# Queue positions of Q's weight loads and of the second gate/up group in a linear-attention and ReGLU block

## The chip, the cores and the metric

The kernel runs on one core of one Trainium2 chip. Its engines work from separate instruction queues: TensorE (PE) multiplies matrices into PSUM, VectorE (DVE) and ScalarE (ACT) take results out of PSUM and do elementwise work, GpSimd (POOL) does elementwise work in SBUF, and SyncE (SP) only issues DMA transfers. Each queue is worked off in the order in which it was written; an engine that waits holds everything behind it. The metric is the device time of one execution in microseconds (us); smaller is better.

## The reference

One transformer block on 2048 tokens (S) of width 1024 (D), in bf16:

```python
x = A_x
h = x + _A_ref(_layernorm(x), A_wqkv, A_wo)
h2 = h + _B_ref(_layernorm(h), B_W_gate, B_W_up, B_W_down)

# _A_ref: 32 heads of 32, linear attention, phi(t) = (t + 1 if t > 0 else exp(t)) + 1e-6
q, k, v = split(x @ wqkv)
kv  = einsum("sd,se->de", phi(k), v)          # per head, summed over all tokens
z   = sum over tokens of phi(k)
o   = (phi(q) @ kv) / (phi(q) @ z + 1e-6)
return o @ wo

# _B_ref
return (relu(x @ W_gate) * (x @ W_up)) @ W_down     # width 3584 inside
```

K and V of all tokens must be known before the first token's attention can be computed; Q is first needed after that.

## The kernel before

**Products.** The large products are written as Strassen-like quads (`Quad`): a two-by-two block product in seven half-size products m = 1 to 7 instead of eight, in Winograd's form. Each needs sums and differences of the blocks of both operands. Those of the weights are made by `WForms.sums` (four DVE subtractions of 128 x 2048 elements for each of K, V and Q; m = 4 to 7 use them) and, for gate and up, by `GW.sums` (four of 128 x 1024 elements); those of the activations by `left_sums`. A quad's own copies and additions (`fork`, `snap`, and the functions in its `out` table) fall to ACT and DVE.

**Stages.**
1. x is loaded in 16 tiles of 128 tokens. `Norm` computes mean and variance of a tile (on DVE for one half, on ACT for the other), scales it on POOL (`finish`, line 677) and has SP transpose it by a DMA (`dma_start_transpose`, line 682) into `XI`. The first two tiles, 0 and 8, are transposed on TensorE instead, so SP transposes 14 tiles of x.
2. The loop of line 868 runs over token pairs p = 1 to 7 (tiles p and p + 8): a quad for K, one for V, and the accumulation of kv and z (`kv_acc`). The norm of the tiles of pair p + 2 is started in the background of pair p (line 872), so tiles 7 and 15 are started in pair 5.
3. The Q quads (`q_quad`) follow: four for token half-block s = 0 and four for s = 1. `Tile_` computes attention for a tile of tokens: `group` the division, with an x tile loaded again for the residual and a DMA transpose of o at its end; `wo` the output product and the residual sum; `norm` (line 1033) the second layer norm, whose normalized tile `hn` is again transposed by SP into `XI` (line 1041). There are eight such tiles in each of s = 0 and s = 1, so 32 transposes in this stage.
4. Gate and up (`gu_halves`, then `gu_quad`) run over `order` (line 1188): `n` counts its entries, the first four of which are s = 0 with weight columns fc = 0 to 3. Gate and up weights come in groups of two columns fc, four DMAs each of 512 KB (`load_group`). Group 0 is loaded ahead of the Q quads; group 1, for fc = 2 and 3, is written in the source behind the first entry's quads (line 1239) and goes into memory in which Q's weights stood, half of it free once the second Q quad of s = 1 is done and the other half after the fourth.
5. The down product follows from spilled and reloaded operands, to the end.

**Order.** No engine runs the source's order. `Plan` records every operation as a node with the nodes whose data it needs (`preds`), the time that it holds its engine, and its latency. `order` works out for every node how late it may start (`late`); `schedule` then goes through model time and gives each engine, whenever it is free, the one of its ready nodes with the smallest `late` (TensorE: the earliest in source order within a window). A node that has no urgent use is thus taken early when its engine is free in the model and its inputs are there. A load is ready as soon as its memory is free, and up to 120 us ahead of its `late`; a load that isn't urgent is held only until the model's wire is free:

```python
if v.late - max(clock[e], v.ready) > 6000.0:
    v.ready = max(v.ready, wire - 2000.0)
```

The queue of SP comes out of this too, and so does the place of the weight differences among DVE's other work. On the chip the order of each queue is fixed; the waits between engines come from the data alone.

**Names that the change touches.** `Plan.take` makes the nodes. `W_ORDER` and `WQ.load(k, h)` are the four loads of Q's weights, 512 KB each; in the source they stand at line 875, after K's quad of p = 3. `WQ.sums()`, Q's four differences, is put in the background at p = 6 (line 873).

Of the kernel before, what the change touches and what calls it, by code (L numbers as in the profile page):

```python
# [32 lines left out]
class Plan:  # L33
# [12 lines left out]
    class Engine:  # L46
        def __init__(self, plan, name):
            self._plan, self._name = plan, name
# [3 lines left out]

    def __init__(self, nc):
        self.nc, self.nodes, self.state, self.cache = nc, [], {}, {}
        for e in ("tensor", "vector", "scalar", "gpsimd", "sync"):
            setattr(self, e, Plan.Engine(self, e))

# [33 lines left out]
    def cost(self, eng, op, out, ins, k):  # L91

        n = self.free(out)
        if eng == "tensor":
            return max(n / 2.4, 98.0) if op == "matmul" else 80.0, 160 + self.SEM
        if op == "dma_start" and eng == "gpsimd":
            return 1000.0, 2.0 * self.wire(out) + 4500.0
        if op == "dma_start" and eng == "gpsimd":
            return 1000.0, 2.0 * self.wire(out) + 2500.0
        if eng == "sync":  # L100
            return (1250.0, 2350.0) if op == "dma_start_transpose" else (500.0, self.wire(out) + 2200.0)
        acc = 85.0 if k.get("accum_out") is not None else 0.0
        psum = any(a.space == PSUM for a in ins)
        if eng == "vector":
            narrow = all(self.nbytes(a) == 2 and a.space != PSUM for a in (out, *ins) if self.free(a) > 1)
            mode = {"tensor_tensor": 2, "tensor_scalar": 4, "memset": 2}.get(op, 1) if narrow else 1
            if ins:
                n = max(n, self.free(ins[0]))
            return n / (0.96 * mode) + 69 + acc, 95 + self.SEM
        if eng == "scalar":  # L110
            return n / 1.2 + (51 if psum else 93) + 2 * acc, 105 + self.SEM
        return n * 1.15 + 100, 60 + self.SEM

    def take(self, eng, op, args, k):
        outs, ins = [], []
        for i, a in list(enumerate(args)) + list(k.items()):
            if hasattr(a, "ap") and hasattr(a, "offset"):
                (outs if i in (0, "out", "accum_out") else ins).append(a)
        out = outs[0]
        accumulates = k.get("accum_op") is not None or op == "matmul" and not k.get("start", True)  # L120
        nodes = self.nodes
        call = lambda: getattr(getattr(self.nc, eng), op)(*args, **k)  # L122
        hold, lat = self.cost(eng, op, out, ins, k)
        if nodes and nodes[-1].open and op == "matmul":
            v = nodes[-1]
            v.hold += hold
        else:
            v = Plan.Node()
            v.eng, v.calls, v.preds, v.hold, v.lat, v.dma = eng, [], set(), hold, lat, 0.0
            if op == "dma_start":  # L130
                v.dma = self.wire(out) * (2.0 if eng == "gpsimd" else 1.0)
            nodes.append(v)
        v.calls.append(call)
        v.open = op == "matmul" and not k.get("stop", True)
        me = len(nodes) - 1
        for a in ins + (outs if accumulates else []):
            if a.space == DRAM and a.tensor.name.startswith("in_"):
                continue
            name, gs = self.granules(a)
            last, readers = self.state.setdefault(name, ({}, {}))  # L140
            for q in gs:
                w = last.get(q)
                if w is not None:
                    v.preds.add(w)
                readers.setdefault(q, set()).add(me)
        for a in outs:
            name, gs = self.granules(a)
            if eng == "tensor" and not accumulates:

                per = 2048 // self.G  # L150
                gs = [per * b + i for b in sorted({q // per for q in gs}) for i in range(per)]
            last, readers = self.state.setdefault(name, ({}, {}))
            for q in gs:
                w = last.get(q)
                if w is not None:
                    v.preds.add(w)
                r = readers.pop(q, None)
                if r:
                    v.preds |= r
                last[q] = me  # L160
        v.preds.discard(me)

    def cut(self):

        if self.nodes:
            self.nodes[-1].open = False
# [128 lines left out]
def chain_of(*fs):  # L295

    if not fs:
        return None

    def f():  # L300
        fs[0]()
        return chain_of(*fs[1:])

    return f
# [155 lines left out]
def block_kernel(ctx: ExitStack, tc: tile.TileContext, x, wqkv, wo, wg, wu, wd, out, H: int):  # L460
    nc = tc.nc
# [8 lines left out]
    ST = S // P  # L470
# [77 lines left out]
    hw, nc = nc, Plan(nc)  # L548
# [12 lines left out]
    W_ORDER = ((0, 0), (1, 0), (0, 1), (1, 1))  # L561
# [28 lines left out]
    WK, WV, WQ = WForms(84, D), WForms(112, 2 * D), WForms(56, 0)  # L590
# [34 lines left out]
    class Norm:  # L625
# [51 lines left out]
        def finish(self):  # L677
            self.rstd_()
            xn = self.xn
            nc.gpsimd.tensor_scalar(out=xn, in0=self.x, scalar1=self.negm[:], scalar2=self.rstd[:],  # L680
                                    op0=ALU.add, op1=ALU.mult)
            nc.sync.dma_start_transpose(out=XI[self.i][:, :, self.r:self.r + P], in_=xn)
            if self.t % NP + 2 < NP:
                load_x(self.t + 2)

# [182 lines left out]
    for p in range(1, NP):  # L868
        pk, kq = k_quad(p)
        if p > 1:  # L870
            q = 3 if p == 2 else p + 2
            tick.bg.extend([norm(q), None, norm(q + NP, True)] if q < NP else
                           [None, *WQ.sums()] if p == NP - 2 else [])
        qs.run(kq)
        if p == 3:
            for k, h in W_ORDER:
                WQ.load(k, h)
        v, vq = v_quad(p)
        ls = left_sums((p + 1) % NP * P, P)
        if p == 2:  # L880
            tick.bg.extend([norm(p + 2), norm(p + 2 + NP, True), None] + ls)
        else:
            tick.bg.extend(([None] * 3 if p == 1 else [None]) + ls)
        qs.run(vq)
        kv_acc(*pend.pop(0))
        pend.append((p, pk, v))
# [29 lines left out]
    def load_group(g):  # L916
        w = groups[g] = at(W_A[g], [2, KC, 2, 2 * P])
        for y, v in enumerate((wg_v, wu_v)):
            for h in range(2):
                nc.sync.dma_start(out=w[:, y, :, h, :], in_=v[:, :, h, g * 2 * P:(g + 1) * 2 * P])  # L920
# [42 lines left out]
    class Tile_:  # L963
# [69 lines left out]
        def norm(self):  # L1033
            lnv = scratch("lnv2", 1)
            nc.scalar.activation(out=lnv[:], in_=self.ss[:], func=ACT.Ln, bias=LN_EPS, scale=1.0 / D)
            rstd = scratch("rstd2", 1)
            nc.scalar.activation(out=rstd[:], in_=lnv[:], func=ACT.Exp, scale=-0.5)
            nc.gpsimd.tensor_scalar(out=self.hn, in0=self.h, scalar1=self.negm[:], scalar2=rstd[:],
                                    op0=ALU.add, op1=ALU.mult)
            c = slice(self.s * SW + self.tt * P, self.s * SW + (self.tt + 1) * P)  # L1040
            nc.sync.dma_start_transpose(out=XI[self.i][:, :, c], in_=self.hn)
            if self.i == 1 and (self.tt == 1 or self.tt > 1):
                n = 2 if self.tt == 1 else 1
                return (lag_s[0], chain_of(*left_sums(self.s * SW + (self.tt + 1 - n) * P, n * P)))

    lag_s = [3]
    tiles = [Tile_(s, i, tt) for s in range(NS) for tt in range(SW // P) for i in range(2)]

    def w(m, j):
# [16 lines left out]
    NTS = len(tiles) // 2  # L1066
# [162 lines left out]
    for n, (s, fc) in enumerate(order):  # L1229
        gw = forms[fc]  # L1230
        if n == 4:
            quads.flush()
            tick.drain()
        next_forms(n + 1)
        if n < 4:
            for q in gu_halves(s, fc, gw, five_banks):
                quads.run(q)
            if n == 0:
                load_group(1)
        else:  # L1240
            quads.run(gu_quad(s, fc, gw, four_pairs))
        if n in loads:
            load_group(loads[n])
        if 8 <= n < 8 + FH:
            wd_sums(n - 8)
        if 9 <= n < 13:
            spill(0, n - 9)
        if n == 24:
            r1 = at(164, [2, FQ, DW])
            for k in range(2):  # L1250
                nc.sync.dma_start(out=r1[:, k, :, :], in_=wd_pairs[:, 0, :, k, 0:DW])
            z1 = l1_part(0, 12)
        elif n == 26:
            z1 += l1_part(12, FH)
# [278 lines left out]
```

## Time and profile before

| | us |
|---|---|
| median of 4 runs | 728.9 |
| lowest and highest run | 728.73, 729.85 |
| the profiled execution's own time | 728.73 |
| its span in the profile | 727.0 |

The span is the time from the first to the last instruction in the trace; the 1.7 us beside it lie around it. Durations below are from this execution. In the profile's rows nearly all instructions stand under L122, the line through which `Plan` issues them, so they are told apart by engine, shape and tile names: `mem` is the one SBUF buffer, `psum` the PSUM banks, `tiny` small per-token values, `in_..._dram` the inputs. SPq rows are DMA issues: their length is the time that SP's queue was held, not the transfer's.

The stages by time, as the rows of TensorE, DVE and SP show them:

| us | stage |
|---|---|
| 0 to 22 | first loads, plain products of tiles 0 and 8 |
| 22 to 118 | K and V quads, p = 1 to 7 |
| 118 to about 195 | Q quads, and attention for s = 0 from 147 on |
| 195 to about 265 | gate and up begin, attention for s = 1 beside them |
| to 727 | gate, up and down |

Mean busy share of the 16 DMA engines in the 40 slices of 18.2 us begins with 9 9 5 5 2 0 4 5 2 3 9 9 tenths. From 74 to 87 us it is 0.22, from 87 to 113 us 0.01 or less.

### The profile page before, as it was taken

How to read it: one execution, taken by the hardware profiler on the slowest of the kernel's cores; microseconds unless marked ns; L12 is line 12 of the kernel's file. 1: busy time of each engine (PE TensorE's matmuls, PEld its weight loads, DVE VectorE, ACT ScalarE, POOL GpSimd, SP SyncE). 2: the span in 40 equal slices, each digit the busy share in tenths (PEclk: the TensorE clock that was granted, in tenths of full speed). 3: DMA queues.
4: the chain of work that ended last, by engine and by line, in shares of the span. 5: the costliest groups of instructions: out<-in, count | busy, mean ns of one | idle time of the engine just before them, and what ended most of it. 6: DMA issues, size and time to landing. Idle time of an engine off the chain costs nothing.

```text
span 727.0 us, 11235 instructions
## 1 busy us (share of the span) xinstructions
PE 715.1 (98%) x4163; PEld 396.9 (55%) x4163; DVE 563.0 (77%) x949; ACT 279.7 (38%) x544; POOL 80.5 (11%) x90
## 2 busy tenths in 40 slices
PE   8999999999999999999999999999999999999998
PEld 3444445444444444444444444444444688888887
DVE  6997645896897785575767968759668878999996
ACT  5778545666555443323333333333333220001100
POOL 2433000002202120000000000000000004101452
PEclk9999999999999999999999999999999999999999
DMA  9955205239945730456156485685592878877973
GB/s 306 242 119 120 40 1 168 66 79 245 197 104 146 145 87 0 123 147 180 51 147 195 151 250 163 189 254 180 160 290 70 267 260 200 229 272 236 235 88 59
DMA packets 156503, 117.40 MB, mean 161 GB/s; under 512 B 54944, under 2 KB 140192, under 8 KB 156320
## 3 DMA queue, kind: packets, MB, share of 16 engines
q1 hardware_dynamic: 148832, 113.01, 54.2%
q0 software_dynamic: 7616, 3.67, 4.7%
q8 instruction: 32, 0.52, 0.3%
q14 instruction: 23, 0.19, 0.1%
HBM read 70.52 MB, written 34.08 MB: 144 GB/s over the span
## 4 chain that ended last, share of the span: by engine, by line
PE 86%; DVE 5%; DMA 3%; ACT 3%; issue 1%; POOL 0%; SPq 0%; ACTq 0%; DVEq 0%
PE psum L122 86%; DVE mem L122 4%; ACT mem L122 3%; DMA mem<-mem 2%; DMA mem<-in_A_x_dram 1%; DVE tiny L122 0%; POOL mem L122 0%; SPq L122 0%; ACT tiny L122 0%; ACT psum L122 0%; ACTq L122 0%; DVEq L122 0%
## 5 line engine op out<-in xcount | busy, mean ns | idle before, releaser
L122 PE MATMUL psum<-mem 128*128 128x512 f16 (+4 forms) x4147 | 714.2, 335 | 7.9 <-ACT mem L122 3.3
L122 PEld LDWEIGHTS <-mem 128*128 128x128 f16 (+1 forms) x4163 | 396.9, 98 | 326.3 <-issue 9.5
L122 DVE TENSOR_TENSOR mem<-psum,mem 128x512 f32<-128x512 f32 (+2 forms) x240 | 187.3, 793 | 100.5 <-ACT mem L122 64.7
L122 DVE TENSOR_TENSOR mem<-mem 128x512 f16<-128x512 bf16 (+8 forms) x400 | 241.6, 644 | 15.5 <-DMA mem<-mem 7.9
L122 ACT COPY mem<-psum 128x512 f32<-128x512 f32 (+2 forms) x124 | 92.8, 750 | 210.8 <-PE psum L122 205.9
L122 ACT COPY psum<-psum 128x512 f32<-128x512 f32 (+1 forms) x68 | 49.1, 722 | 161.6 <-PE psum L122 159.5
L122 POOL DMA_DIRECT2D out_dram<-mem x28 | 34.1, 1302 | 413.8 <-DVE mem L122 413.7
L122 POOL TENSOR_SCALAR mem<-mem,tiny 128x1024 bf16<-128x1024 bf16 x30 | 39.6, 1321 | 196.4 <-ACT tiny L122 173.9
L122 ACT ACTIVATE mem<-psum 128x512 bf16<-128x512 f32 x90 | 53.8, 597 | 17.0 <-PE psum L122 16.4
L122 DVE SCALAR_TENSOR_TENSOR mem<-mem 128x512 bf16<-128x512 bf16 (+1 forms) x71 | 58.6, 825 | 1.3
L122 DVE SCALAR_TENSOR_TENSOR mem<-psum,mem 128x512 bf16<-128x512 f32 x66 | 45.4, 688 | 11.9 <-PE psum L122 7.9
L122 ACT ACTIVATE mem<-mem,tiny 128x1024 bf16<-128x1024 bf16 x25 | 28.6, 1145 | 10.6 <-DVE tiny L122 5.8
L122 DVE TENSOR_SCALAR mem<-mem 128x512 bf16<-128x512 bf16 (+1 forms) x49 | 16.4, 335 | 20.7 <-ACT mem L122 20.5
L122 ACT ACTIVATE mem<-mem 128x1024 bf16<-128x1024 f32 (+1 forms) x24 | 25.3, 1055 | 5.8 <-DVE mem L122 5.7
L122 DVE TENSOR_TENSOR mem<-psum,tiny 128x384 bf16<-128x384 f32 (+1 forms) x48 | 22.9, 508 | 5.3 <-ACT tiny L122 3.9
L122 ACT ACTIVATE tiny<-tiny 128x1 f32<-128x1 f32 (+2 forms) x112 | 22.7, 206 | 9.1 <-DVE tiny L122 6.3
L122 ACT ACTIVATE tiny<-psum 128x12 f32<-128x12 f32 (+1 forms) x48 | 8.2, 170 | 13.8 <-PE psum L122 13.4
L122 ACT CAST mem<-psum 128x512 bf16<-128x512 f32 x18 | 10.5, 582 | 2.8 <-PE psum L122 2.1
L122 DVE BATCH_NORM_STATS2 tiny<-mem 128x6 f32<-128x512 bf16 x14 | 9.0, 677 | 2.4 <-DMA mem<-in_A_x_dram 2.4
L122 POOL TENSOR_SCALAR tiny<-tiny 128x1 f32<-128x1 f32 x14 | 5.3, 378 | 25.7 <-ACT mem L122 18.1
L122 ACT ACTIVATION_READ_ACCUMULATOR mem<-mem,tiny 128x1 f32 x25 | 4.7, 189 | 0.0
L122 DVE TENSOR_SCALAR tiny<-tiny 128x1 f32<-128x1 f32 x16 | 3.4, 210 | 0.3
(18 smaller groups left out, 13.5 us busy)
## 6 DMA issues: line engine op xcount, KB each, us to landing
l_dram<-mem SPq DMA_DIRECT2D x98, 128.0 KB, 2.2
mem<-l_dram SPq DMA_DIRECT2D x12, 896.0 KB, 6.0
mem<-in_A_x_dram SPq DMA_DIRECT2D x32, 256.0 KB, 3.1
mem<-in_B_W_up_dram SPq DMA_DIRECT2D x14, 512.0 KB, 5.1
mem<-in_B_W_gate_dram SPq DMA_DIRECT2D x14, 512.0 KB, 4.1
mem<-in_B_W_down_dram SPq DMA_DIRECT2D x28, 256.0 KB, 3.7
r_dram<-mem SPq DMA_DIRECT2D x56, 128.0 KB, 2.0
mem<-r_dram SPq DMA_DIRECT2D x8, 896.0 KB, 5.2
```

The source lines that it names most:

```text
L122: call = lambda: getattr(getattr(self.nc, eng), op)(*args, **k)
```

## The change

`Plan` gets a field `behind`. While it is set to a node, every node of SP that is recorded has that node among its predecessors; with `chain` set, which no call does here, each would also follow the one before. `follow(node)` sets it and `follow(None)` ends it; `last()` is the number of the newest node. Nothing is added to the instructions: it constrains where the planner puts a DMA issue in SP's queue.

It is used twice. The loads of Q's weights are taken from line 875 and recorded in `Norm.finish` of the last tile, 15, right after its transpose, which they follow. `load_group(1)` stays where it is in the source, and its four loads follow the eighth transpose of `hn`, the last one of s = 0, whose number is kept in the new list `turned`. A second branch of `cost` with the condition of the first goes.

```diff
@@ Plan.__init__
+        self.behind = None
@@ Plan.cost
-        if op == "dma_start" and eng == "gpsimd":
-            return 1000.0, 2.0 * self.wire(out) + 2500.0
@@ Plan.take
+        if eng == "sync" and self.behind is not None:
+            v.preds.add(self.behind)
+            if self.chain:
+                self.behind = me
         v.preds.discard(me)
+
+    def follow(self, node, chain=False):
+
+        self.behind, self.chain = node, chain
+
+    def last(self):
+        return len(self.nodes) - 1
@@ Norm.finish
             nc.sync.dma_start_transpose(out=XI[self.i][:, :, self.r:self.r + P], in_=xn)
+            if self.t == ST - 1:
+                nc.follow(nc.last())
+                for k, h in W_ORDER:
+                    WQ.load(k, h)
+                nc.follow(None)
@@ the loop over p
-        if p == 3:
-            for k, h in W_ORDER:
-                WQ.load(k, h)
@@ Tile_.norm
             nc.sync.dma_start_transpose(out=XI[self.i][:, :, c], in_=self.hn)
+            turned.append(nc.last())
...
-    lag_s = [3]
+    lag_s, turned = [3], []
@@ the loop over order
             if n == 0:
+                nc.follow(turned[NTS - 1])
                 load_group(1)
+                nc.follow(None)
```

## The prediction

> **What bounds the kernel now.** The page comes first. TensorE is busy 715.1 of 727.0 us, its clock row is full in all 40 slices, and the chain that ended last is mostly its matmuls. So a gain can only come out of TensorE's gaps, 12 us in all with the start.
>
> ```profile
> span 727.0 us, 11235 instructions
> PE 715.1 (98%) x4163; PEld 396.9 (55%) x4163; DVE 563.0 (77%) x949; ACT 279.7 (38%) x544; POOL 80.5 (11%) x90
> ```
>
> Where are the gaps? The timeline of TensorE, 10 to 80 us: start, length, what, and in brackets the idle time before it and who ended it.
>
> ```profile
> 22.44 7.08 PE L122 MATMUL psum<-mem 128*128 128x512 bf16 x32 [0.81 <-DMA mem<-mem]
> 29.77 13.23 PE L122 MATMUL psum<-mem 128*128 128x512 f16 x72 [0.25 <-ACT mem L122]
> 44.12 1.02 PE L122 MATMUL psum<-mem 128*128 128x512 f16 x4 [1.12 <-ACT mem L122]
> 45.80 33.66 PE L122 MATMUL psum<-mem 128*128 128x512 bf16 x188 [0.66 <-DVE mem L122]
> 79.68 0.59 PE L122 MATMUL psum<-mem 128*128 128x512 bf16 x2 [0.21 <-DVE mem L122]
> ```
>
> Each gap is about 0.16 us longer than the bracket when counted from start to start against the 0.213 us of an undisturbed 512-column matmul: 0.98, 0.42, 1.29, 0.82 and 0.38, and two of 0.25 inside the long row near 71 and 72 us. That is 4.4 us up to 80 us. From 79.68 to 152 us there is none worth naming; from 152 to 212 us three remain (0.78, 1.30, 0.56 in brackets), then 512 us without a break.
>
> What moves? The timeline of SP's queue, x's part and the first h transposes:
>
> ```profile
> 13.44 0.42 SPq L122 DMA_DIRECT2D mem<-in_A_wqkv_dram  x1
> 18.24 1.35 SPq L122 DMA_TRANSPOSE mem<-mem  x1
> ...
> 22.44 1.52 SPq L122 DMA_DIRECT2D mem<-in_A_wqkv_dram  x3
> ...
> 72.10 1.24 SPq L122 DMA_TRANSPOSE mem<-mem  x1
> ...
> 175.20 0.40 SPq L122 DMA_DIRECT2D mem<-in_B_W_gate_dram  x1
> ...
> 192.59 0.40 SPq L122 DMA_DIRECT2D mem<-in_B_W_up_dram  x1
> 197.59 1.24 SPq L122 DMA_TRANSPOSE mem<-mem  x1
> 199.98 0.38 SPq L122 DMA_DIRECT2D mem<-in_B_W_gate_dram  x1
> 203.73 0.37 SPq L122 DMA_DIRECT2D mem<-in_B_W_up_dram  x1
> ```
>
> Twelve wqkv loads are issued by 24 us; the last four, at 13.44 and 22.44, are Q's. They are 50 to 60 us ahead of the last x transpose (72.10). And DVE's groups by shape, 29.2 to 46 us, show what they draw after them:
>
> ```profile
> L122 DVE TENSOR_TENSOR mem<-mem 128x2048 f16<-128x2048 bf16 x4 | 5.4, 1380 | 0.0
> ```
>
> Only the weight differences have 2048 columns: four for K, four for V, four for Q. The first eight are over by 26.7 us; these four are Q's, at 30.96 (1.90 us), 34.30 and 35.46 (2.37 together) and 43.05 (1.17). Q needs them only after the K/V stage, whose closing mask product stands at 122.23.
>
> **Q's loads, the first to be issued.** The load at 13.44 took 8.1 us to land, so it was on the wire until 21.5. The transpose at 18.24 landed after 4.16 us; undisturbed ones (31.82, 40.05, 45.69) take 3.0 to 3.1. Without the load it lands 1.1 us earlier, at 21.3, and the gap at 22.44 closes. But little of that is kept: twelve matmuls on (22.44 + 12 x 0.213 = 25.0) TensorE needs sums of the next transposed block. That transpose, issued at 20.50, landed at 23.98; DVE's two sums at 23.98 (0.42) and 24.43 (0.42) end at 24.85, and the first f16 weights load at 24.91, after a wait of 0.20 on DVE. POOL hands the block over only at 20.47, so this does not move. TensorE would come 0.94 us earlier and wait 0.85. Kept: **0.1 us**; bounds 0 and 0.9. ACT, however, gets its first copy 0.9 us sooner and is busy without a break from 24 to 31, so the 0.42 gap at 29.77, which waits for an ACT copy at 29.13 behind two normalization passes, should close: **0.4 us**.
>
> **Q's four differences.** They cannot run before their loads, so they leave the stretch 29 to 46, in which DVE has 0.2 us idle beside 1 us of waits on ACT. Does TensorE feel it? The 1.29 gap at 44.12 ends with an ACT copy at 43.51. ACT had stood still before:
>
> ```profile
> 43.16 0.44 ACT L122 ACTIVATE tiny<-tiny 128x1 f32<-128x1 f32 x2 [1.25 <-DVE tiny L122]
> ```
>
> It waited for the variance that DVE finished at 43.13 (42.92 + 0.21), and DVE reached those statistics at 41.62 with 1.90 + 1.23 + 1.21 = 4.3 us of Q's differences ahead of them. The 0.82 gap at 45.80 waits for DVE's addition at 45.07, behind these and the fourth difference at 43.05. With 5.4 us gone, 4.3 of it before 42 us, a delay of 1.3 and then 0.8 us has no cause. What is late next is ACT (9.8 of 13 us busy from 35 to 48) and the matmuls themselves; neither asks for 1 us. Kept: **2.1 us**; bounds 0.5 (ACT holds the place) and 2.1.
>
> **Where they go.** Behind the transpose at 72.10 SP is free at 73.35. Four issues of about 0.5 us follow; nothing on SP is behind them but a residual load (73.50), first used near 156. The wire is empty: DMA share 0.22 from 74 to 87 us, 0.01 after. A 512 KB load on a quiet wire landed in 3.6 to 4.5 us (203.73, 175.20), and the three at 22.44 landed 1.45 us apart, so I estimate landings at 77.5, 79, 80.4 and 81.9. Q's first product is at about 118, so 36 us are left. The differences now stand in DVE's queue between evictions of K and V, where DVE idles 18 us of 38 (80 to 118), in pieces of 1.0 to 2.5 us. 4 x 1.2 us fit. If one stands there before its load has landed, everything behind it on DVE waits: the clamps and joins that free the PSUM banks. The trace has two such stalls, at 70.00 (2.44 us, on a transpose) and 77.00 (2.20): they cost TensorE 0.5 and 0.4 us. Bounds: 0 for no stall; for a stall until the last landing at 81.9, nearly 7 us from 75, so 7 - 2 = 5 us. I take a stall of 1.5 us, which by those rows is **0.3 us lost**, because the row at 22.44 shows differences placed well after landings (28.2 to 31.1 against 30.96 to 43.05).
>
> [...] By the rows 36 us of cover are left where 4.5 to 8.1 are needed, so lateness costs nothing, and the early landing is what puts 5.4 us onto a full DVE. [...]
>
> **Second group.** Two of its four loads already stand behind the eighth hn transpose (197.59); two move from 175.20 and 192.59 to about 199. The first had delayed the oT transpose at 176.00, which landed after 4.5 instead of 3.1 us and held SP 1.92 instead of 1.24. But TensorE runs from 153.48 to 194.18 without a gap, so this cover hides it: 0. The gap at 195.48 comes from the hn transpose at 185.80 (4.8 us to land, DVE idle 2.60 until 190.61). POOL gave it up at 185.78 and the 175.20 load had landed at 179.7, so it stays. The new issues (4 x 0.4 us) fit between 198.83 and SP's next work at 209.71. Landing at about 207 is what the 203.73 load already did, and DVE's first difference from that group is at 214.96. Cost 0; bounds -0.5 to +0.5, since the order of the attention stage may come out differently by less than a gap. The deleted second branch could never be reached, and the new fields issue no instruction: 0.
>
> **The sum.** -0.1 - 0.4 - 2.1 + 0.3 = -2.3 us against the profiled execution's 728.73 (span 727.0 and 1.7 around it), 726.4. The median of the four runs is 0.17 higher, so I say 726.5.
>
> **Rivals.**
> *ACT takes DVE's place* (0.25). For it: from 24 to 31 and 35 to 48 ACT is nearly full, and the gap at 44.12 ends with ACT. Against: it sat idle 1.25 us just there, waiting for DVE. Then 0.5 us is won: 728.4.
> *Q's differences stand before their loads* (0.16). Place: DVE, 75 to 82 us. Price: stall less the 2 us that the two observed stalls show to be covered. It decides from a stall of 4.7 us, where 2.7 is lost against 2.6 won; at 7 us the time is 728.73 - 2.6 + 5 = 731.1. For it: DVE already waited for transposes at 70 and 77, so its order there assumes earlier landings than it gets. Against: the differences are not urgent for 36 us.
> *It does not do what it says*: if another x transpose were issued after the one tied to, the loads could collide with it; the price is the 1.1 us of the transpose at 18.24 with 10 us of lead, so nothing. It falls within the first two.
>
> **Numbers.** Forecast 0.59, its own range 725.0 (the 0.9 us of gaps between 70 and 80 also close, and 0.6 in the attention stage) to 727.4. A measurement tells from no change about 0.2%, 1.5 us: below 727.4 is faster, above 730.4 slower. So faster 0.59, same 0.25, slower 0.16. The range 724.9 to 729.8 takes in the first rival and leaves out the second and a little below.
>
> **What would show it.** Right: wqkv issues after the last x transpose near 71; the 128x2048 differences between 77 and 118; no TensorE gap over 0.5 us between 30 and 47; the first gap moved from 22.44 to just before 25 and hardly shorter; first h transposes undisturbed near 176. Wrong: gaps at 44 and 46 still there with ACT busy ahead of them; DVE idle on in_A_wqkv for several us near 80 with a TensorE gap after it; or the gaps of 152 to 212 us larger than 2.6 us in brackets, which would mean that the attention stage was reordered at a cost that I put at nothing.

## The result and the profile after

The changed kernel takes 727.6 us (median of 41 runs, 725.8 to 729.3) against 729.0 us (62 runs of the kernel before beside them). The ratio is 0.9978 with a 95% interval of 0.9972 to 0.9984: 1.6 us less, between 1.2 and 2.0 (the two medians themselves lie 1.4 apart). The profiled execution took 728.0 us.

The first rows of its page, the span and the engines (busy time, share, instructions):

```profile
span 726.2 us, 11233 instructions
PE 714.5 (98%) x4163; PEld 396.7 (55%) x4163; DVE 562.8 (78%) x949; ACT 279.3 (38%) x544; POOL 80.1 (11%) x90
```

The span is 0.8 us shorter, and TensorE does the same 4163 matmuls. The timeline of TensorE, 10 to 262 us (start, length, what, idle time before it and who ended it):

```profile
21.94 2.76 PE L121 MATMUL psum<-mem 128*128 128x512 bf16 x12 [0.22 <-DMA mem<-mem]
26.76 125.05 PE L121 MATMUL psum<-mem 128*128 128x512 f16 x682 [2.06 <-DVE mem L121]
152.59 40.70 PE L121 MATMUL psum<-mem 128*128 128x512 bf16 x219 [0.79 <-DMA mem<-mem]
194.72 9.26 PE L121 MATMUL psum<-mem 128*128 128x512 bf16 x48 [1.43 <-ACT mem L121]
204.53 57.75 PE L121 MATMUL psum<-mem 128*128 128x132 bf16 x304 [0.56 <-DVE mem L121]
```

From 26.76 on 682 matmuls follow one another: the gaps at 29.77, 44.12, 45.80 and 79.68 are gone. The gap before the first quad shrank from 0.98 to 0.39 us, start to start. But twelve matmuls later stands a gap that the kernel before does not have: 2.22 us, ended by DVE. The rows from 152 us on are the old ones.

Summed over each stretch, TensorE's time lost against undisturbed spacing, one matmul every 0.213 us (in us):

| | 12 to 30 | 30 to 60 | 60 to 100 | 100 to 215 | sum |
|---|---|---|---|---|---|
| before | 1.59 | 2.27 | 1.04 | 4.69 | 9.59 |
| after | 2.81 | 0.21 | 0.92 | 4.82 | 8.76 |
| moved by | +1.22 | -2.06 | -0.12 | +0.13 | -0.83 |
| forecast | -0.5 | -2.1 | +0.3 | 0 | -2.3 |

The sum agrees with the spans. SP's timeline of the changed kernel shows what was moved:

```profile
18.72 1.36 SPq L121 DMA_TRANSPOSE mem<-mem  x1
21.91 1.24 SPq L121 DMA_TRANSPOSE mem<-mem  x1
...
71.33 1.24 SPq L121 DMA_TRANSPOSE mem<-mem  x1
72.61 3.29 SPq L121 DMA_DIRECT2D mem<-in_A_wqkv_dram  x4
...
196.83 1.24 SPq L121 DMA_TRANSPOSE mem<-mem  x1
198.12 0.57 SPq L121 DMA_DIRECT2D mem<-in_B_W_gate_dram  x1
198.78 0.58 SPq L121 DMA_DIRECT2D mem<-in_B_W_up_dram  x1
```

Q's four loads stand directly behind the last transpose of x, and the second group starts behind the hn transpose at 196.83. DVE's timeline has Q's four differences one at a time, the first and the last of them here:

```profile
80.46 1.22 DVE L121 TENSOR_TENSOR mem<-mem 128x2048 f16<-128x2048 bf16 x1
...
91.24 1.22 DVE L121 TENSOR_TENSOR mem<-mem 128x2048 f16<-128x2048 bf16 x1
```

No wait of DVE on Q's weights appears between 74 and 118 us. And the chain that closed the 44-us gap before, DVE's statistics to ACT, no longer has a wait in ACT's timeline:

```profile
43.13 0.43 ACT L121 ACTIVATE tiny<-tiny 128x1 f32<-128x1 f32 x2
43.50 0.59 ACT L121 COPY mem<-psum 128x512 f32<-128x512 f32 x1
```

Earlier, behind the new gap, it is ACT that waits for TensorE:

```profile
27.83 0.59 ACT L121 COPY mem<-psum 128x512 f32<-128x512 f32 x1 [1.77 <-PE psum L121]
```

So the loss in DVE's full stretch went as foreseen, and 1.22 of the 2.06 us came back at the start. The experiments ask what each part does, and where the new gap comes from. All of them are timed; a ratio is to the kernel before on the same chip.

### The profile page after: what moved, and what is told of

It reads as the page before. It is cut to its first block, busy times and chain, and to the rows that moved or that the text cites. A ratio compares the mean times of both kernels' runs of the same rounds, so it can differ in the third digit from the quotient of the medians.

```text
span 726.2 us, 11233 instructions
## 1 busy us (share of the span) xinstructions
PE 714.5 (98%) x4163; PEld 396.7 (55%) x4163; DVE 562.8 (78%) x949; ACT 279.3 (38%) x544; POOL 80.1 (11%) x90
## 4 chain that ended last, share of the span: by engine, by line
PE 85%; DVE 2%; DMA 2%; ACT 1%; issue 0%; POOL 0%; ACTq 0%
PE psum L121 85%; DVE mem L121 2%; DMA mem<-mem 2%; ACT mem L121 1%; POOL mem L121 0%; ACT tiny L121 0%; DVE tiny L121 0%; ACTq L121 0%
## 5 line engine op out<-in xcount | busy, mean ns | idle before, releaser
L121 ACT ACTIVATE mem<-mem 128x1024 bf16<-128x1024 f32 (+1 forms) x24 | 25.4, 1056 | 6.6 <-DVE mem L121 6.6
L121 DVE TENSOR_TENSOR mem<-psum,tiny 128x384 bf16<-128x384 f32 (+1 forms) x48 | 22.9, 508 | 5.3 <-ACT tiny L121 3.9
```

## The experiments: which part does it

**One part alone.** `q_loads_only` is the changed kernel with the second group left where it was:

```diff
             if n == 0:
-                nc.follow(turned[NTS - 1])
                 load_group(1)
-                nc.follow(None)
```

> The change without its second part: Q's loads and with them Q's four differences move, the second gate and up group stays. Theory A (the gain is DVE's relief between 30 and 46 us, the second group is worth nothing): as the whole change, ratio 0.9978 within 0.0007, gaps before 44 and 46 us gone. Theory B (the second group's loads carry the gain): 1.000. In the profile the first gap, near 22, and the one of 2.06 us near 26.8 may differ from those of the changed kernel, since nothing that was changed acts before 18 us: if the gap near 26.8 is a matter of chance, it is between 0 and 2.2 us here.

`group_only` is the kernel before with only this second part:

```diff
             if n == 0:
+                nc.follow(turned[NTS - 1])
                 load_group(1)
+                nc.follow(None)
```

> The kernel before with only the loads of the second gate and up group moved. Theory A: no change, ratio 1.000 within 0.0007; the oT transpose near 176 us lands in 3.1 instead of 4.5 us and TensorE shows no difference. Theory B: 0.998.

Measured: `group_only` 1.0008 (0.9997 to 1.002), with the gaps before 44 and 46 us in place (2.27 us lost from 30 to 60, as before). The second part does nothing that can be measured: in `group_only` the oT transpose at 177.05 us lands after 3.4 us, where it took 4.5 before, and TensorE's rows there do not move. `q_loads_only` has the gain from 30 to 60 (0.21 us lost) and the new gap (3.32 us lost from 12 to 30), but its ratio is 0.9999 (0.9985 to 1.0013), not that of the whole change. Its order of work up to 118 us is the changed kernel's, instruction for instruction, so the Q part carries the gain in the trace, and something at the start takes it away in the time. This is taken up below.

**The differences without the loads.** In `differences_only` the loads of Q stay early and only Q's four differences are held until behind the last x transpose:

```diff
@@ Plan.take
+        if eng == "vector" and self.held is not None:
+            v.preds.add(self.held)
@@ the loop over p
+    def held(f):
+        def g():
+            nc.held = x_last[0]
+            f()
+            nc.held = None
+        return g
...
-                           [None, *WQ.sums()] if p == NP - 2 else [])
+                           [None, *map(held, WQ.sums())] if p == NP - 2 else [])
```

> The kernel before with Q's loads where they were; only Q's four differences on DVE are held back in the order until behind the last transpose of x. Theory A (DVE's relief): gaps before 44 and 46 us gone, 2.1 us there, and the whole ratio 0.9975 to 0.9985, like the change. Theory C (the wire: loads ahead of transposes): the gaps stay and the ratio is 1.000; the transpose near 18.2 us still lands after 4.2 us.

Measured: 0.9994 (0.9985 to 1.0003). TensorE's loss from 30 to 60 us falls to 0.55 us, of which 0.42 is the gap on ACT that stood at 29.77 before and is at 30.64 here, with every load on the wire as before: it was DVE's 5.4 us, not the traffic. The gain is lost again further on. TensorE's and then DVE's timeline:

```profile
78.49 6.22 PE L121 MATMUL psum<-mem 128*128 128x512 bf16 x28 [0.30 <-DVE mem L121]
86.28 34.08 PE L121 MATMUL psum<-mem 128*128 128x512 bf16 x192 [1.57 <-DVE mem L121]
```

```profile
78.35 3.48 DVE L121 TENSOR_TENSOR mem<-mem 128x512 f16<-128x512 f16 x5
81.75 0.68 DVE L121 TENSOR_TENSOR mem<-psum,mem 128x512 bf16<-128x512 f32 x1
82.35 2.35 DVE L121 TENSOR_TENSOR mem<-mem 128x2048 f16<-128x2048 bf16 x2
```

Here the planner put two differences in a row (82.35, 2.35 us) ahead of the evictions, and TensorE stood 1.74 us at 86.28. In the changed kernel all four stand singly and cost nothing. One difference between evictions was covered, two were not; this rests on one trace of each order.

**One load back.** `first_load_early` is the changed kernel with the first of Q's four loads at its old place, near 14 us:

```diff
@@ Norm.finish
-                for k, h in W_ORDER:
+                for k, h in W_ORDER[1:]:
@@ the loop over p
+        if p == 3:
+            WQ.load(*W_ORDER[0])
```

> The whole change, except that the first of Q's four loads stays where it was, issued near 13.4 us; the other three follow the last transpose of x. DVE's order is nearly that of the change. It puts the wire's share apart: theory A says that the first load costs nothing that is kept, as TensorE waits for the second transposed block anyway: ratio as the change, 0.9978 within 0.0007, the transpose near 18.2 us back at 4.2 us and the gap near 22.4 back at 0.8. Theory C: 0.5 to 0.9 us slower than the change, 0.9985 to 0.9991.

Measured: 0.9970 (0.9959 to 0.9982), 727.3 us; span 725.8. Neither theory had foreseen a gain over the whole change. The new gap is gone. TensorE's timeline:

```profile
23.57 7.08 PE L121 MATMUL psum<-mem 128*128 128x512 bf16 x32 [1.62 <-DMA mem<-mem]
30.89 17.28 PE L121 MATMUL psum<-mem 128*128 128x512 f16 x91 [0.25 <-ACT mem L121]
```

The first transposed block lands after 4.1 us again, TensorE starts its first quad later than the changed kernel does, and then runs through: 1.98 us lost from 12 to 30 instead of 2.81, and 0.55 from 30 to 60, of which 0.42 is the gap on ACT at 30.89. The start differs from trace to trace: the gap before the first quad is 0.98 us in the trace of the kernel before, and 1.7 to 1.8 in the four other traces with this load early and the full warm-up unchanged. So the fairest pair is `q_loads_only` and `first_load_early`, whose first transposes are issued at 19.48 and 19.41. Without the load the first gap is 0.84 instead of 1.79, which is the 0.94 that the prediction counted on, and the gap behind it is 2.28 instead of none: 1.3 us more lost. So it is the load at 13.44, the one that I counted as a gain of 0.1 us, whose removal costs time.

## The experiments: where the new gap comes from

The gap ends with DVE's sums of the second transposed block (tile 9). The forecast had 0.85 us of waiting there; what is late beyond that is the block. Two things delay it. In the profiled execution after, POOL handed it over 3.19 us behind the first block instead of 2.26 (transposes at 18.72 and 21.91, before at 18.24 and 20.50), because a small operation that took 0.23 us in the kernel before took 1.44. ACT stood 1.00 us behind it, and the value that POOL needs for the second block came later by way of ACT. POOL's and ACT's timelines of the changed kernel, then POOL's of `q_loads_only`:

```profile
13.24 1.44 POOL L121 TENSOR_SCALAR tiny<-tiny 128x1 f32<-128x1 f32 x1 [10.79 <-ACT mem L121]
```

```profile
14.71 1.15 ACT L121 ACTIVATE mem<-mem,tiny 128x1024 bf16<-128x1024 bf16 x1 [1.00 <-POOL tiny L121]
```

```profile
14.59 0.23 POOL L121 TENSOR_SCALAR tiny<-tiny 128x1 f32<-128x1 f32 x1 [12.14 <-ACT mem L121]
```

At 13.22 DVE had begun a weight difference of 2048 columns, beside it; in `q_loads_only` POOL's operation began 0.22 us ahead of DVE's. That the two belong together was not tested. `q_loads_only` has no such delay, and the same gap:

```profile
22.70 2.77 PE L121 MATMUL psum<-mem 128*128 128x512 bf16 x12 [0.68 <-DMA mem<-mem]
27.58 20.60 PE L121 MATMUL psum<-mem 128*128 128x512 f16 x106 [2.12 <-DVE mem L121]
```

So POOL is a chance of the execution (`change_third`, the same program as the changed kernel, is without the delay too) and not the cause common to all. What the traces have in common is a late landing of the transpose itself. The DMA view of the changed kernel, 22.9 to 24.1 us, shows what is on the wire beside it (queue: packets, MB, share; and the issue with its time to landing):

```profile
q8 instruction: 1, 0.02, 5.1%
...
mem<-mem SPq DMA_TRANSPOSE x1, 3.9
```

In `first_load_early` the view from 22.9 to 25.2, the whole rest of the transpose, has no such packet, and the one from 25.4 to 26.6 has it:

```profile
mem<-mem SPq DMA_TRANSPOSE x1, 3.4
```

```profile
q8 instruction: 1, 0.02, 5.0%
```

It is one packet of 16 KB of instructions, about 1 us on one of the 16 DMA engines (5.1% of the sixteen over 1.2 us). The traces of all kernels with the same warm-up, with the packet placed to half a microsecond:

| kernel | Q's first load | second transpose issued | lands after | packet | against the transpose |
|---|---|---|---|---|---|
| before | early | 20.50 | 3.5 | 24.5 to 25.0 | behind |
| group_only | early | 21.25 | 3.6 | 25.5 to 26.0 | behind |
| differences_only | early | 21.42 | 3.4 | 25.5 to 26.0 | behind |
| first_load_early | early | 21.66 | 3.4 | 25.5 to 26.0 | behind |
| first_early_again | early | 21.23 | 3.4 | 25.5 to 26.0 | behind |
| after | late | 21.91 | 3.9 | 23.0 to 23.5 | on it |
| change_again | late | 21.76 | 4.2 | 22.5 to 23.0 | on it |
| q_loads_only | late | 21.74 | 4.9 | 24.5 to 25.0 | on it |
| change_third | late | 21.71 | 4.9 | 24.0 to 24.5 | on it |

(`change_again` and `change_third` are repetitions of the changed kernel, `first_early_again` of `first_load_early`; they follow.) Whose instructions are they? The page counts 32 such packets. TensorE executes 2 x 4163 instructions, 260 for each packet, and from one packet to the next it does 186 to 311 over all traces; in these nine the first comes at its 189th to 200th instruction. My reading of these counts, which no view states, is that TensorE's own program comes in these packets: a TensorE that starts its first quad earlier would then also get its packet earlier, on top of the transpose that it will wait for next. Part of it stays unexplained: in `q_loads_only` TensorE starts 1.0 us earlier against the second transpose than in the kernel before, but the packet comes 1.5 us earlier.

The place within the transpose matters, as the start times of all packets in the thirteen kept traces show. Of 51 transposes on which a packet began 1.0 to 2.49 us after their issue, all landed after 3.85 us or more, half of them after 4.6 or more. Of 488 without a packet, 20 did, and the median was 3.1. But ten transposes of x near 50 us were issued within 0.25 us of a packet's start and landed after 3.02 to 3.19 us, as if it were not there, and near 262 us a packet that began 2.5 to 2.9 us after the issue changed nothing either (3.05 to 3.2), while at 2.7 to 2.9 us near 22 us (`q_loads_only`, `change_third`) the landing took 4.9.

**Moving the packet.** By this reading extra TensorE instructions at the start should move the packet and nothing else. `first_early_10_more` is `first_load_early` with ten more matmuls of 64 columns on zeros in the warm-up; nothing reads their results.

```diff
+        for _ in range(2):
+            nc.nodes[-1].calls.append(lambda b=b: hw.tensor.matmul(
+                bank(b)[:, 0:64], lhsT=junk[:, 0:P], rhs=junk[:, 0:64], start=True, stop=True))
```

> The kernel with Q's first load kept early, with 10 matmuls of 64 columns on zeros added behind the warm-up ones (never read), all else in the same order. Instruction packets are called for 20 instructions earlier, about 2.1 us: the one at 25.9 us should come near 24, onto the second transpose. Theory F: that transpose takes 4 us or more, a gap of 1 to 2 us opens between 25 and 29 us, and the run is 1 to 2 us slower than first_load_early, ratio about 0.999. Theory G: as first_load_early, 0.997.

The other direction, with ten of the fifteen warm-up matmuls left out, was run for the changed kernel (`change_10_fewer`) and for `first_load_early` (`first_early_10_fewer`):

```diff
-        for _ in range(3):
+        for i in range(3):
...
+            if i > 0:
+                nc.nodes[-1].calls.clear()
```

> The changed kernel with 10 of the 15 warm-up matmuls on zeros left out as instructions (their output is never read); every other instruction is in the same order. All later TensorE instructions stand 20 places nearer to the front, so a 16 KB instruction packet, some 260 instructions, is called for 20 instructions, about 2.1 us, later in the work. Theory F: the packet that came at 23.0 to 24.6 us comes near 25 to 27, the second transpose lands after 3.1 to 3.6 us, the gap near 26.8 falls from 2.2 to below 1 us, and the run is 1 to 1.5 us faster than the changed kernel. Theory G or a cause in DVE or POOL: no difference near 26.8.

> The kernel with Q's first load kept early and 10 of the 15 warm-up matmuls left out as instructions. Theory F: nothing to win near 25 us, where the packet was already behind the second transpose; it moves from 25.9 to about 28, which may hit the third transpose, issued near 29.7, not at all. Ratio 0.997 as first_load_early, or a little under if the packets near 73 and 188 us also miss the transposes there (up to 1.5 us for the gap before 195 us).

And the changed kernel once more beside them:

> The changed kernel itself, a second profile of it on this chip. Theory F (the gap of 2.2 us near 26.8 us is made by the change: with the first Q load gone TensorE starts on the first transposed block earlier, so the 16 KB instruction packet that its progress calls for reaches the wire while the second transpose is on it): the gap is there again, the packet starts within the second transpose's time, that transpose takes 3.9 us or more, and the ratio is about 0.998. Theory G (it was chance in one execution): the gap is absent or much smaller.

Measured with ten more: the packet moved from 25.5 to 20.0, farther than foreseen, onto the first transpose instead of the second. The first then landed after 6.1 us instead of 4.1, the second after 5.5 instead of 3.4. TensorE's timeline and the DMA view from 20 to 21.4 us:

```profile
24.39 7.08 PE L121 MATMUL psum<-mem 128*128 128x512 bf16 x32 [2.90 <-DMA mem<-mem]
```

```profile
q8 instruction: 1, 0.02, 4.6%
...
mem<-mem SPq DMA_TRANSPOSE x1, 5.5
```

The second is late with the first: it lands 1.5 us behind it, as in the kernel before. The gap before the first quad grew from 1.79 to 3.07 us with no change in any load or in the order of the other work. So in this trace the transpose that the packet was moved onto took 2.0 us longer. The loss of time that I expected did not come: 0.9972 (0.9964 to 0.9979), as without the extra matmuls. What a packet on a transpose costs in time is therefore not shown by this. The packet came at TensorE's 189th instruction once more, the twenty extra ones counted in; it moved so far because TensorE now reaches that number before its wait for the first transposed block and not after it.

With ten fewer the test failed. The packet came at 25.0 and 24.5 us, about the old place, and the warm-up was spoiled: the granted clock was half, with matmuls 0.43 us apart, until 17 us in `change_10_fewer` and until 13 us in `first_early_10_fewer` (full from 5.9 us on in the changed kernel), as in this row of `change_10_fewer`, where eight take 3.62 us (1.89 in the changed kernel):

```profile
8.51 3.62 PE L121 MATMUL psum<-mem 128*128 128x512 bf16 x8
```

Both kernels were no faster than before (1.0008 each; 1.0001 to 1.0014 and 1.0000 to 1.0016). One thing they show all the same: far on, near 188 us, another packet falls onto an hn transpose in every kernel with the full warm-up, and its landing after 4.1 to 5.1 us ends in the gap of 1.0 to 1.6 us near 195 that I had left as it is. Here the packet missed it, as it does in `first_early_5_fewer` below, where the gap is 0.21 us too. The transpose in question and TensorE's row, first after, then `first_early_10_fewer`:

```profile
mem<-mem SPq DMA_TRANSPOSE x1, 4.9
...
194.72 9.26 PE L121 MATMUL psum<-mem 128*128 128x512 bf16 x48 [1.43 <-ACT mem L121]
```

```profile
mem<-mem SPq DMA_TRANSPOSE x1, 3.1
...
195.22 9.26 PE L121 MATMUL psum<-mem 128*128 128x512 bf16 x48 [0.21 <-ACT mem L121]
```

**What the gap costs in time.** `change_again` gave 0.9987 (0.9977 to 0.9996), and its profiled execution a span of 728.7. Its windows after the gap (TensorE's busy time and matmuls, weight loads, DVE, ACT, POOL, granted clock, DMA share, GB/s):

```profile
24.00:27.00 3.00, 0.62 (x4) 0.13 (x3) 2.26 (x5) 1.88 (x5) 0.48 (x1) 1.00 0.52 132
27.00:31.00 4.00, 4.00 (x11) 1.45 (x12) 3.78 (x7) 2.30 (x5) 1.53 (x2) 0.57 0.00 0
31.00:35.00 4.00, 4.00 (x20) 1.86 (x19) 1.91 (x4) 2.75 (x8) 1.00 (x1) 1.00 0.56 131
```

In these 4 us behind the gap (2.54 us here) the mean granted clock is 0.57, since it is half for 3.41 us of them: 11 matmuls instead of 20, some 1.7 us (half of the 3.41). Whether this may have happened in a run can be read from its mean granted clock, since 1.7 us of 727 are 0.0023: I take a run at 0.998 or less as one with such a dip. Where in the run it lay is known for the profiled executions alone. Three last kernels were run for the question whether this and the choice of the load decide: `first_early_again`, the changed kernel as `change_third`, and `first_early_5_fewer`, `first_load_early` with five of the warm-up matmuls left out (as above with `i > 1`).

> The kernel with Q's first load kept early once more, beside the changed kernel on the same chip. Theory F (the change's own loss at the start): again no gap near 27 us, second transpose 3.4 us, 0.7 to 1.5 us faster than the changed kernel of this call, ratio to before about 0.997. Otherwise the two are equal within 0.1%.

> The changed kernel, for comparison in this call: ratio 0.998 to 0.999, the gap of 2.2 to 2.5 us near 27 us there for the third time, the second transpose landing after 3.9 us or more. Where the gap is at its longest, matmuls behind it may start 0.43 instead of 0.21 us apart, as in the second profile.

> The kernel with Q's first load kept early and 5 of the 15 warm-up matmuls left out as instructions. Theory F: the instruction packet near 187 us, which made the h transpose issued near 184.5 land after 4.8 us, moves by about 10 instructions; if it leaves that transpose, it lands after 3.1 us, the gap before 194 us falls from 1.5 to 0.4 and the run is 1 us faster than first_early_again: 0.9955 to 0.996. If it moves too little, 0.997. If 10 warm-up matmuls are too few, matmuls near 13 us start 0.43 us apart and the run is slower than first_early_again by 1 to 2 us.

Measured on one chip: 0.9965 (0.9953 to 0.9977) for the first load early and 0.9990 (0.9981 to 1.0000) for the changed kernel, 726.5 and 728.3 us, as theory F had it, though 1.8 us apart and not 0.7 to 1.5, and 0.9979 (0.9963 to 0.9996) for five fewer. The runs by their mean clock:

| kernel | runs at 0.998 or less | their median, us | the others' median, us |
|---|---|---|---|
| after, change_again, change_third | 7 of 42, 5 of 13, 4 of 11 | 729.1, 729.4, 729.5 | 727.5, 727.8, 728.0 |
| q_loads_only | 7 of 11 | 730.2 | 728.4 |
| first_load_early, first_early_again | 0 of 6, 0 of 5 | | 727.3, 726.5 |
| first_early_10_more | 0 of 20 | | 727.4 |
| first_early_5_fewer | 6 of 12 | 729.9 | 725.8 |

The two kernels with ten warm-up matmuls fewer are left out, as the half clock until 17 and 13 us lowers their mean clock too. Without the new gap such runs are rare: 2 of 107 of the kernel before whose clock is on record and 2 of 11 of `group_only`, and these, at 732.5 to 733.3 us, must have lost more or elsewhere. With the new gap they are 23 of 77 (first two rows of the table), at medians 1.5 to 1.8 us above the others'. Divided by the median of the kernel before beside them, the other runs of the changed kernel give 0.998 all three times, so the share of dips accounts for most of why the same kernel gives 0.9978, 0.9987 and 0.9990, and for most of why `q_loads_only` gives 0.9999: more of its eleven runs have one. The 0.6 us by which its other four runs are above the changed kernel's are not explained. Five fewer warm-up matmuls give the lowest single times (725.3), and the gap near 195 us is closed as foreseen. But there is a gap of 2.42 us before 28.35, half of the runs have a low clock, and the profiled execution, at 0.995, has two dips, one of them at 8.5 us in the warm-up, so this is no improvement.

With Q's first load early and the other three late the kernel is faster than the kernel before and than the change: 0.9970 and 0.9965 on two occasions, against 0.9978 to 0.9990 for the change.

## Why the prediction came out as it did

The predicted 726.5 us is 1.1 below the median measured (its own sum and the 0.17 make 726.6). The forecast, faster through Q's differences leaving DVE's full stretch, is what happened, but weaker: 727.6 lies 0.2 above the line of 727.4 that the prediction drew for faster, and above its own range. By its steps:

- **Q's four differences, "Kept: 2.1 us".** The loss from 30 to 60 us fell by 2.06. That it is DVE is shown by `differences_only`, which has the same relief with the loads in place. The first rival, ACT in DVE's place, would have kept 0.5; it is refuted.
- **Where they go, "0.3 us lost".** Nothing was lost (-0.12): no difference stood ahead of its load. The second rival did not occur. `differences_only` shows that this place has a price all the same, but for two differences in a row ahead of evictions, 1.74 us, and not for a load that is late, which is what I had looked at.
- **The ACT gap at 29.77, "0.4 us".** Gone, but not for the reason given. ACT was to be busy without a break there; instead it stood 1.77 us before its copy at 27.83, waiting for TensorE, which came late out of the new gap. Where the new gap is missing, in `first_load_early`, this one is still there with 0.42. The number was luck.
- **Q's loads, the first to be issued, "Kept: 0.1 us; bounds 0 and 0.9".** This is the term that was mis-sized; it is a loss of 1.6 us in the two profiled executions, 1.3 in the pair above. The gap before the first quad shrank by 0.59, and the wait twelve matmuls on came, but at 2.22 instead of 0.85. I had written that the second block "does not move", and excluded a loss on that. In the profiled execution it moved by 0.93 at POOL and by 0.4 on the wire: 0.85 + 0.93 + 0.4 = 2.2. In `q_loads_only` and `change_third` POOL was on time and the transpose took 4.9 instead of 3.5: 0.85 + 1.4 = 2.25, measured 2.28 and 2.27. That TensorE comes about 0.9 earlier was right; that nothing else moves was wrong. Together with the 0.4 above the stretch lost 1.22 where I had it gain 0.5.
- **Second group, "Cost 0".** Measured 0 (`group_only` at 1.0008; the changed kernel's stretch from 100 to 215 us differs by +0.13). The gap at 195 that I left open goes with the same thing as the one at the start, an instruction packet on a transpose: 1.43 us where that transpose landed after 4.9, 0.21 where the packet missed it and it landed after 3.1.
- **"Lateness costs nothing".** For three of the four loads this was right: `first_load_early`, with these three late, is 0.3% faster than before. For the first load it was not, 1.3 us more lost in the pair above, though nobody waits for this load. In the traces with it early TensorE starts its first quad later against the second transpose, and the packet comes 0.8 to 1.0 us behind the landing of the next transpose.

The sum forecast was -2.3 us; the profiled executions differ by 0.75, a third of it, and the ratio of all runs says 1.6 (1.2 to 2.0). The profiled execution after lies 0.4 above its median and the one before 0.3 below that of its 62 runs. So that the time came out nearer than the traces is chance in which executions were profiled, and the sum by steps explains the traces better than the medians.

## What to carry to other kernels

Work with slack is best kept off an engine that is full in a critical stretch, and delaying the load that releases it was enough to do that here, where the planner takes whatever is ready (2.06 us less lost from 30 to 60 us); then look where it reappears, since here one such operation between evictions was free and two cost 1.74 us. When a wait on a path is removed, the next wait on that path must be priced with everything that shifts with it, here a second transpose that landed after 3.9 to 4.9 us instead of 3.4 to 3.6, and not at its old time. And a gap like this one of 2.2 to 2.5 us should be judged by the run-to-run clock as well: here the runs with a mean clock of 0.998 or less took 1.5 to 1.8 us more.

## What the hardware showed that was not expected

**Instruction packets against DMA transposes.** A 16-KB packet of instructions, about 1 us on one DMA engine, goes with a transpose landing after 3.9 to 6.1 us instead of 3.1 to 3.6 where it begins 1.0 to 2.5 us after the transpose was issued, at 23 us, at 20 us, at 188 us and elsewhere. Where one begins with the transpose, near 50 us, the landing took 3.02 to 3.19 us. Why the place matters is not shown. What decides the moment of a packet is only partly understood: with the full warm-up, and with ten matmuls more, the first comes at TensorE's 189th to 200th instruction, but with five and ten fewer at the 178th, 167th and 159th. No run took the packet away with all else the same.

**The clock after a short gap.** In a dip TensorE ran at half rate, 0.43 us from matmul to matmul instead of 0.21, for 3.41 us each time. Within a trace the clock changes only at times that lie a multiple of 3.41 us apart (in `change_again` at 6.85, 27.33 and 30.74; in the kernels before and after it is full for 720.21 us, 211 times 3.413). The length of the gap alone did not decide: gaps of 2.54 and 2.42 us were followed by the half rate in two traces, while gaps of 2.22 to 2.40 in others and one of 3.07 were not. Divided into stretches of 3.41 us that begin and end at such times, the thirteen traces agree with one another: once the clock was full, it fell after each stretch in which TensorE was idle for 2.13 to 2.38 us (three of them, the end of the execution left aside) and after none with 1.90 or less. The gap of 3.07 us was idle for 1.00 us in one stretch and 1.90 in the next, the 2.22 us of the changed kernel for 1.68 and 0.38, and the clock stayed full after both. What lies between 1.90 and 2.13 us, and why the clock falls, these traces do not show.
